# Sliding-window attention with sinks and a SwiGLU block: a range test of the softmax reciprocals and a branch at the end of the program

## The chip, the cores and the metric

The kernel runs on one core of one Trainium2 chip. Times are device microseconds of one launch. A core has five engines with instruction streams of their own: TensorE (PE; its weight loads are listed apart as PEld), VectorE (DVE), ScalarE (ACT), GpSimd (POOL) and SyncE (SP). They wait for each other and for DMA transfers through semaphores. An engine that issues a DMA goes on at once; the transfer raises a semaphore when it has landed.

## What is computed

Attention over 4 batches, 8 heads, 768 positions and heads of 64, in which each query sees the first 4 positions (the sinks) and the last 128 positions up to itself, and then a SwiGLU block on the 3072 resulting rows of 512:

```python
scores = np.where(is_sink | in_window, scale * q @ k.T, -1e9)
a = np.exp(scores - max(scores));  a = a / (sum(a) + 1e-9);  x = a @ v
out = (silu(x @ w_gate) * (x @ w_val)) @ w_out      # 512 -> 1536 -> 512
```

Queries and keys are drawn at a tenth of unit size, so the scores are small. The kernel takes the exponentials without subtracting each row's maximum.

## The kernel before, in words

**Attention** is done in 12 groups of 256 query rows (three per batch). For a group, `step_S` makes the scores, transposed, with their exponentials on ScalarE (L295) and the mask as a product on VectorE (L300); `step_K` makes the sinks' scores (L316). `step_PV` multiplies the exponentials with the values, four heads at a time. The value tiles have a column of ones beside the 64 values of a head, so the sum of the exponentials comes out as the 65th column of the product `po`. `step_PV` then takes the reciprocal of that column (L359: a tile `rcp` of 128x4 from the pool `smallp`, with four buffers) and scales the product by it into `xn` (L365 on VectorE, L362 on ScalarE). `step_X` transposes `xn` into `xT`. There are 48 such reciprocals: 12 groups, two halves of 128 rows, two halves of the heads.

**The SwiGLU block** works on eight row blocks (`SIZES`: 256, 256, 256, 512, 512, 512, 512, 256). `gate` makes one 128x512 piece of the hidden layer: two products on TensorE (L416, tiles `pg` and `pv`), a tanh on ScalarE (L436), two operations on VectorE (L444, L455). `down` makes 128 rows of the output: 12 matmuls (L496, tile `pd`), a copy out of PSUM (L501 on ScalarE; L503 on VectorE for the last 128 columns of the last rows) and a store (L504), which SyncE issues for the later row blocks. PSUM has eight banks, which all tiles of TensorE's results take in turn (`bank`).

**The order** is written out by hand. `weave` goes through a list of `gate` and `down` steps and hands each the attention steps of its slot; `down` spreads what it is handed evenly among its 12 matmuls. Each engine runs its instructions in the order in which this recording makes them. The last list has 24 steps: 12 `gate` steps of row block 6, 6 of row block 7, four `down` of block 6 (steps 18 to 21) and two of block 7. Its attention steps end in slot 9, so steps 10 to 23 are SwiGLU alone.

**The end.** After its last instruction each engine goes to an end block. There SyncE waits, one after the other, for the semaphores of all DMAs and engines; then all engines meet in a barrier, POOL clears the semaphores, and they meet again.

Of the kernel before, what the change touches and what calls it, by code (L numbers as in the profile page):

```python
# [6 lines left out]

FP32 = mybir.dt.float32
BF16 = mybir.dt.bfloat16
AF = mybir.ActivationFunctionType  # L10
ALU = mybir.AluOpType
# [3 lines left out]
def kernel(  # L15
# [12 lines left out]
    nc = tc.nc  # L28
    P = 128
    B, H, S, D = q.shape  # L30
    NS = int(n_sink)
    W = int(window)
    DM = moe_w_gate.shape[0]
# [3 lines left out]
    DMC = DM // P  # L37
    DFC = DF // P
    NP2 = H // 2
    GC = S // 256  # L40
    NG = B * GC
# [6 lines left out]
    FCH = [2] * 6  # L48
    FOF = [(i, f - sum(FCH[:i])) for i in range(len(FCH))
           for f in range(sum(FCH[:i]), sum(FCH[:i + 1]))]  # L50
    scale = 1.0 / float(D) ** 0.5

    def pool(name, bufs, psum=False):
        if psum:
            return ctx.enter_context(
                tc.tile_pool(name=name, bufs=bufs, space=bass.MemoryType.PSUM))
        return ctx.enter_context(tc.tile_pool(name=name, bufs=bufs))

    const = pool("const", 1)
    wpool = pool("wpool", 1)  # L60
    rowp = pool("rowp", 3)
    natp = pool("natp", 1)
    vpool = pool("vpool", 1)
    kqtp = pool("kqtp", 2)
    epool = pool("epool", 2)
    espool = pool("espool", 2)
    xnp = pool("xnp", 4)
    smallp = pool("smallp", 4)
    xtp = pool("xtp", 3)
    tpool = pool("tpool", 3)  # L70
    upool = pool("upool", 3)
    hpool = pool("hpool", 2)
    opool = pool("opool", 4)
# [4 lines left out]
    def bank(shape, dtype, name):  # L78
        return psum.tile(shape, dtype, tag="b", name=name)


    rows, nats, vas = {}, {}, {}
# [43 lines left out]
    wgs, wvs, wos = [], [], []  # L126
# [17 lines left out]
    ident = const.tile([P, P], BF16)  # L144
# [5 lines left out]
    tq = const.tile([P, P], FP32)  # L150
    tk = const.tile([P, 1], FP32)
# [3 lines left out]
    warmed = const.tile([P, 1], FP32)  # L155
    KW = 32
    kss = const.tile([P, B, NP2, KW + 2 * NS], BF16)
    vsbs = []

    nc.vector.memset(zero, 0.0)  # L160
# [45 lines left out]
    def flush():  # L206
        for f in later:
            f()
        later.clear()
# [114 lines left out]
    def step_sinks(g):  # L324

        b, c = divmod(g, GC)
        for j in range(2):
            for hh in range(2):
                r = slice(32 * (2 * j + hh), 32 * (2 * j + hh + 1))
                pos[j, hh] = bank([P, 4, D + 1], FP32, "o")  # L330
                nc.tensor.matmul(pos[j, hh], es_t[g][r], vsbs[b][r], start=True,  # L331
                                 stop=False, skip_group_check=True)

    def step_PV(g, j, hh, norm="v"):
        b, c = divmod(g, GC)
        t = 2 * c + j
        if hh == 0:
            xns[g, j] = xnp.tile([P, DM], BF16, tag="xn", name="xn")
        if c > 0 and j == hh == 0:
            step_sinks(g)  # L340
        po = pos.pop((j, hh)) if c > 0 else bank([P, 4, D + 1], FP32, "o")
        mms = []
        for hq in range(4):
            h = 4 * hh + hq
            if t > 0:
                vp = vas[g][:, 0, h, 0:D + 1] if j else vas[g - 1][:, 1, h, 0:D + 1]
                mms.append((po[:, hq], e_t[g][:, h, 256 * j:256 * j + P], vp))
            mms.append((po[:, hq], e_t[g][:, h, 256 * j + P:256 * (j + 1)],
                        vas[g][:, j, h, 0:D + 1]))
        for i, (o, l, r) in enumerate(mms):  # L350
            nc.tensor.matmul(o, l, r, start=(c == 0 and i == 0),  # L351
                             stop=(i == len(mms) - 1),
                             skip_group_check=True)

        xn = xns[g, j][:, 256 * hh:256 * (hh + 1)].rearrange("p (h d) -> p h d", h=4)

        def dve():
            rcp = smallp.tile([P, 4, 1], FP32, tag="rcp", name="rcp")
            nc.vector.reciprocal(rcp, po[:, :, D:D + 1])  # L359
            if norm == "a":  # L360
                for hq in range(4):
                    nc.scalar.activation(  # L362
                        xn[:, hq], po[:, hq, 0:D], AF.Copy, scale=rcp[:, hq])
            else:
                nc.vector.tensor_tensor(  # L365
                    xn, po[:, :, 0:D], rcp.broadcast_to([P, 4, D]), op=ALU.mult)
        if norm == "a":
            dve()
        else:
            later.append(dve)  # L370
# [135 lines left out]
    def gates(tb):  # L506
        return [(gate, tb, f) for f in range(0, DFC, 512 // SIZES[tb])]
# [4 lines left out]
    def A(fn, *a):  # L512
        return lambda: fn(*a)
# [4 lines left out]
    def Ss(g):  # L518
        return [A(step_S, g, p2) for p2 in range(2)]

    def PVs(g):
        return [A(step_PV, g, j, hh) for hh in range(2) for j in range(2)]

    def Xs(g):
        return [A(step_X, g, j) for j in range(2)]
# [11 lines left out]
    def K(g):  # L537
        return A(step_K, g)

    def weave(us, slots):  # L540
        assert all(i < len(us) for i in slots)
        for i, (fn, tb, x) in enumerate(us):
            fn(tb, x, slots.get(i, []))

    def slots(*pairs):
        sl = {}
        for at, steps in pairs:
            for i, step in zip(at if isinstance(at, tuple) else (at,) * len(steps),
                               steps):
                sl.setdefault(i, []).append(step)  # L550
        return sl
# [106 lines left out]
    later[:0] = masks1  # L658
    flush()

    g0, g1, g2 = gates(0), gates(1), gates(2)
    us = [(gate_held, *g0[0][1:]), (gate_first, *g0[1][1:]), g1[0], g1[1],
          *((gate, "01", f) for f in range(4, DFC)),
# [25 lines left out]
    def pair(ga, gb, sh=0):  # L689
# [15 lines left out]
    us = gates(6) + gates(7) + downs(6) + downs(7)  # L705
    us[-1] = (lambda tb, t, a: down(tb, t, a, True), *us[-1][1:])
    weave(us, slots(
        ((0, 2), Ss(11)), (0, [K(11)]), ((4, 5, 6, 7), PVs(11)), ((8, 9), Xs(11))))


# [33 lines left out]
```

## Time and profile before

| what | value |
|---|---|
| median of 3 runs | 238.3 us (237.76 to 238.68) |
| span of the profiled execution, first to last instruction | 235.8 us (235.84) |
| busy: PE, DVE, ACT, POOL | 229.0, 157.7, 113.6, 74.9 us |
| mean granted TensorE clock | 0.999 |
| L359 reciprocals, 48 | 8.3 us busy, 1.0 us idle before them |
| L496 matmuls | 64.5 us busy |
| instruction packets: q8 / q14 | 15, 0.25 MB / 8, 0.07 MB |

How to read it: the span is one execution seen by the profiler, and the runs are timed without it; no time of the profiled execution is listed other than its span. The page's second part cuts the span into 40 slices with the busy share of each engine in tenths. The chain follows the work that ended last backwards, from each instruction to what released it. A row of the timeline gives the start, the length, the engine, the line, the operation, and how long the engine stood idle before it and for whom. Waits on semaphores, register instructions and branches are not counted as busy; where they are spoken of, the times are those of their records in the same trace, from the span's start.

### The profile page before, as it was taken

How to read it: one execution, taken by the hardware profiler on the slowest of the kernel's cores; microseconds unless marked ns; L12 is line 12 of the kernel's file. 1: busy time of each engine (PE TensorE's matmuls, PEld its weight loads, DVE VectorE, ACT ScalarE, POOL GpSimd, SP SyncE). 2: the span in 40 equal slices, each digit the busy share in tenths (PEclk: the TensorE clock that was granted, in tenths of full speed). 3: DMA queues.
4: the chain of work that ended last, by engine and by line, in shares of the span. 5: the costliest groups of instructions: out<-in, count | busy, mean ns of one | idle time of the engine just before them, and what ended most of it. 6: DMA issues, size and time to landing. Idle time of an engine off the chain costs nothing.

```text
span 235.8 us, 4879 instructions
## 1 busy us (share of the span) xinstructions
PE 229.0 (97%) x1867; PEld 127.7 (54%) x1893; DVE 157.7 (67%) x333; ACT 113.6 (48%) x235; POOL 74.9 (32%) x100
## 2 busy tenths in 40 slices
PE   8999999999999999999999999999999999999994
PEld 5768545795555654444445444445444445488443
DVE  4998888768660988950888970698960598877000
ACT  4884495367453826423836522755522653333221
POOL 8995874724403209105325350080000000000000
PEclk9999999999999999999999999999999999999999
DMA  8999999995995929957989997599414100200132
GB/s 138 165 183 176 182 200 204 159 147 81 166 227 164 148 47 88 156 112 160 137 114 133 137 132 185 126 89 101 81 25 150 50 3 0 45 4 0 48 131 91
DMA packets 108743, 27.62 MB, mean 117 GB/s; under 512 B 95792, under 2 KB 105776, under 8 KB 108720
## 3 DMA queue, kind: packets, MB, share of 16 engines
q0 software_dynamic: 76640, 13.90, 76.4%
q1 hardware_dynamic: 30672, 11.58, 25.4%
q10 hardware_dynamic: 1408, 1.84, 2.5%
q8 instruction: 15, 0.25, 0.5%
q14 instruction: 8, 0.07, 0.1%
HBM read 28.34 MB, written 6.29 MB: 147 GB/s over the span
## 4 chain that ended last, share of the span: by engine, by line
PE 93%; DVE 3%; ACT 1%; issue 1%; DVEq 0%; ACTq 0%
PE pv L416 26%; PE pd L496 26%; PE pg L416 26%; PE o L351 4%; PE s L288 4%; PE w L556 1%; DVE xn L365 1%; PE pt L226 1%; PE o L331 1%; PE pt L572 1%; PE pn L241 1%; PE pk L316 1%; ACT th L436 1%; DVE rcp L359 0%; ACT xn L362 0%
## 5 line engine op out<-in xcount | busy, mean ns | idle before, releaser
L444 DVE SCALAR_TENSOR_TENSOR u<-th,pg 128x512 bf16<-128x512 f32 x72 | 49.2, 683 | 39.2 <-ACT th L436 39.2
L416 PE MATMUL pg<-xT,wg 128*128 128x512 bf16 (+1 forms) x353 | 73.5, 336 | 0.7
L436 ACT ACTIVATE th<-pg 128x512 f32<-128x512 f32 x72 | 43.5, 604 | 63.0 <-PE pg L416 58.2
L416 PE MATMUL pv<-xT,wv 128*128 128x512 bf16 (+1 forms) x349 | 72.9, 336 | 0.6 <-ACT e L295 0.2
L496 PE MATMUL pd<-wo,ht 128*128 128x512 bf16 (+2 forms) x292 | 64.5, 371 | 0.5 <-issue 0.2
L416 PEld LDWEIGHTS <-wg 128*128 128x128 bf16 x360 | 35.0, 98 | 27.9 <-issue 0.4
L455 DVE TENSOR_TENSOR ht<-u,pv 128x512 bf16<-128x512 bf16 x62 | 42.7, 688 | 9.4 <-PE pv L416 2.5
L295 ACT ACTIVATE e<-s 128x512 bf16<-128x512 f32 (+1 forms) x88 | 42.8, 581 | 3.9 <-PE s L288 3.7
L496 PEld LDWEIGHTS <-ht 128*128 128x128 bf16 x300 | 27.9, 98 | 30.3 <-issue 0.3
L416 PEld LDWEIGHTS <-wv 128*128 128x128 bf16 x360 | 32.1, 97 | 20.4 <-issue 1.6
L501 ACT ACTIVATE ot<-pd 128x512 f32<-128x512 f32 (+1 forms) x24 | 14.3, 596 | 46.7 <-PE pd L496 40.7
L111 POOL DMA_DIRECT2D nat<-in_k_dram x20 | 17.7, 890 | 39.7 <-DMA qT<-nat 35.8
L300 DVE TENSOR_TENSOR e<-e,mask 128x1024 bf16<-128x1024 bf16 (+1 forms) x44 | 27.2, 653 | 3.7 <-ACT e L295 3.7
L122 POOL DMA_DIRECT2D va<-in_v_dram x24 | 21.5, 919 | 5.5 <-DMA wo<-in_moe_w_out_dram 2.5
L365 DVE TENSOR_TENSOR xn<-o,rcp 128x256 bf16<-128x256 f32 x44 | 18.7, 424 | 1.5
L351 PEld LDWEIGHTS <-e 128*128 128x128 bf16 x352 | 15.0, 98 | 7.9 <-issue 0.2
L111 POOL DMA_DIRECT2D nat<-in_q_dram x20 | 17.7, 899 | 1.1 <-DMA wg<-in_moe_w_gate_dram 0.5
L351 PE MATMUL o<-va,e 128*128 128x65 bf16 x352 | 17.1, 194 | 0.1
L288 PE MATMUL s<-qT,kT 64*128 64x128 bf16 (+1 forms) x240 | 12.9, 238 | 0.0
L288 PEld LDWEIGHTS <-kT 64*128 64x128 bf16 x240 | 7.7, 94 | 7.3 <-issue 6.4
L503 DVE TENSOR_SCALAR ot<-pd 128x128 f32<-128x128 f32 x1 | 0.3, 292 | 14.3 <-PE pd L496 14.3
L359 DVE RECIPROCAL rcp<-o 128x4 f32<-128x4 f32 x48 | 8.3, 175 | 1.0 <-PE o L351 0.9
(74 smaller groups left out, 93.7 us busy)
## 6 DMA issues: line engine op xcount, KB each, us to landing
out_dram<-ot SPq DMA_DIRECT2D x17, 256.0 KB
va<-in_v_dram POOLq DMA_DIRECT2D x24, 128.0 KB, 6.4
nat<-in_k_dram POOLq DMA_DIRECT2D x20, 128.0 KB, 4.4
nat<-in_q_dram POOLq DMA_DIRECT2D x20, 128.0 KB, 5.9
wg<-in_moe_w_gate_dram POOLq DMA_DIRECT2D x6, 256.0 KB, 7.8
wv<-in_moe_w_val_dram POOLq DMA_DIRECT2D x6, 256.0 KB, 8.4
wo<-in_moe_w_out_dram POOLq DMA_DIRECT2D x4, 384.0 KB, 11.1
out_dram<-ot ACTq DMA_DIRECT2D x6, 256.0 KB
```

Source lines behind the costliest of these rows:

```text
L111: nc.gpsimd.dma_start(x[:, i, j].rearrange("p (h d) -> p h d", d=D), src[b, :, t0:t0 + P].rearrange("h p d -> p h d"))
L122: nc.gpsimd.dma_start(va[:, j, :, 0:D], v[b, :, t0:t0 + P].rearrange("h p d -> p h d"))
L288: nc.tensor.matmul(pss[2 * pp + h][:, col:col + n], kTs[b][r, p, kk:kk + P], qTs[b][r, p, qq:qq + n], start=True, stop=True)
L295: nc.scalar.activation(e_t[g][:, h0 + h, lo:512], pss[2 * pp + h][:, lo:512], AF.Exp, scale=scale)
L300: nc.vector.tensor_tensor(e, e, m[:, :, lo:512].broadcast_to([P, 2, 512 - lo]), op=ALU.mult)
L351: nc.tensor.matmul(o, l, r, start=(c == 0 and i == 0), stop=(i == len(mms) - 1), skip_group_check=True)
L365: nc.vector.tensor_tensor(xn, po[:, :, 0:D], rcp.broadcast_to([P, 4, D]), op=ALU.mult)
L416: nc.tensor.matmul(ps[:, i * n:(i + 1) * n], ws[fi][:, c, fo * P:(fo + 1) * P], xTs[tb][:, c], start=(c == 0), stop=(c == DMC - 1))
L436: nc.scalar.activation(th, pg, AF.Tanh, scale=0.5)
L444: nc.vector.scalar_tensor_tensor(u, th, 1.0, pg, op0=ALU.add, op1=ALU.mult)
L455: nc.vector.tensor_tensor(hts[tb][:, f:f + 512 // SIZES[tb]].rearrange("p a n -> p (a n)"), u, pv, op=ALU.mult)
L496: nc.tensor.matmul(po, hts[tb][:, f, ts * P:(ts + 1) * P], wos[f // n][:, f % n, lo:hi], start=(f == 0), stop=(f == DFC - 1))
```

## The change

The reciprocals go into one table, `rcps`, of 128 x 48 x 4 numbers that lives through the whole program; the pool `smallp` is gone. A new step, `guard`, stands in slot 19 of the last list, which is the second `down` of row block 6, so ahead of its seventh matmul. It clips the 192 reciprocals of each partition to the range from 2^-16 to 2^16, compares with the unclipped, takes the minimum over the row (1 where all are in range), sums over the partitions with a product with a column of ones, and writes 1 into `flag` if the sum is under 127.5. After the last `down`, all engines read `flag` into a register and branch. If it is set, `general` computes the whole output anew in loops over batches and tiles of 128 rows, with each row's maximum taken off the scores; else nothing more is done. In the built program, the loops' instructions stand between the branch's other arm (which holds waits and a jump) and the end block.

```diff
+from concourse.expressions import smax, smin
...
-    smallp = pool("smallp", 4)
...
+    rcps = const.tile([P, 4 * NG, 4, 1], FP32)
+    flag = const.tile([P, 1], mybir.dt.int32)
...
         def dve():
-            rcp = smallp.tile([P, 4, 1], FP32, tag="rcp", name="rcp")
+            rcp = rcps[:, 4 * g + 2 * j + hh]
             nc.vector.reciprocal(rcp, po[:, :, D:D + 1])
...
+    LIM = 2.0 ** 16
+
+    def guard():
+
+        n = 16 * NG
+        x = rcps.rearrange("p g h o -> p (g h o)")
+        c = tpool.tile([P, 512], FP32, tag="th", name="clip")
+        ok = upool.tile([P, 512], BF16, tag="u", name="ok")
+        nc.vector.tensor_scalar(
+            c[:, 0:n], x, 1.0 / LIM, LIM, op0=ALU.max, op1=ALU.min)
+        nc.vector.tensor_tensor(c[:, 0:n], c[:, 0:n], x, op=ALU.is_equal)
+        nc.vector.tensor_reduce(ok[:, 0:1], c[:, 0:n], mybir.AxisListType.X, op=ALU.min)
+        ones = vas[0].rearrange("p j h v -> p (j h) v")[:, :, D]
+        n1 = bank([P, 1], FP32, "n")
+        nc.tensor.matmul(
+            n1[0:2 * H], ones, ok[:, 0:1], start=True, stop=True, skip_group_check=True)
+        nc.vector.tensor_scalar(flag[0:1], n1[0:1], P - 0.5, None, op0=ALU.is_lt)
+
+    def general():
...
+        with tc.For_i(0, B) as b:
+            with tc.For_i(0, S // P) as t:
+                tile_general(b, t, idf, bias)
+
+    def tile_general(b, t, idf, bias):
...
     weave(us, slots(
-        ((0, 2), Ss(11)), (0, [K(11)]), ((4, 5, 6, 7), PVs(11)), ((8, 9), Xs(11))))
+        ((0, 2), Ss(11)), (0, [K(11)]), ((4, 5, 6, 7), PVs(11)), ((8, 9), Xs(11)),
+        (19, [guard])))
+
+    with tc.If(nc.values_load(flag[0:1, 0:1], min_val=0, max_val=1) != 0,
+               preferred_fallthrough_block=False):
+        general()
```

## What the change was expected to do, before it ran

> **What bounds the kernel now.** I read the page's first two parts, then its chain, then the tail of the merged chain in order of time, and last the records of SyncE around the end.
>
> ```profile
> PE 229.0 (97%) x1867; PEld 127.7 (54%) x1893; DVE 157.7 (67%) x333; ACT 113.6 (48%) x235; POOL 74.9 (32%) x100
> ...
> PE   8999999999999999999999999999999999999994
> ...
> PEclk9999999999999999999999999999999999999999
> ...
> q8 instruction: 15, 0.25, 0.5%
> q14 instruction: 8, 0.07, 0.1%
> ...
> PE 93%; DVE 3%; ACT 1%; issue 1%; DVEq 0%; ACTq 0%
> ```
>
> TensorE is busy in every slice and holds 93% of the chain, so whatever adds PE time adds to the span at full price, and whatever sits on another engine costs nothing until the last matmul. The last slice is the exception: PE drops to 4. The end of the program is a stretch of its own, and the change puts its wait there.
>
> The chain in order of time, its last two rows, and VectorE and SyncE in the last 19 us:
>
> ```profile
> 217.57 10.74 PE pd L496 x49
> 228.37 4.52 PE pd L496 x32
> ```
> ```profile
> 217.10 0.69 DVE L444 SCALAR_TENSOR_TENSOR u<-th,pg 128x512 bf16<-128x512 f32 x1 [0.27 <-ACT th L436]
> 217.89 0.69 DVE L455 TENSOR_TENSOR ht<-u,pv 128x512 bf16<-128x512 bf16 x1
> 232.91 0.29 DVE L503 TENSOR_SCALAR ot<-pd 128x128 f32<-128x128 f32 x1 [14.34 <-PE pd L496]
> ```
> ```profile
> 220.56 13.01 SPq L504 DMA_DIRECT2D out_dram<-ot  x7
> ```
>
> From 217.1 on only the six output projections run. VectorE is empty from 218.58 to 232.91. PE ends near 232.9, L503 at 233.2, and SyncE issues the last store (record at 233.23, 0.335 long, so to 233.57). The 2.27 us from there to 235.84 are the end block. Its records on SyncE: six waits on DMA semaphores that pass at once, one per 0.062 us (233.61 to 233.92); a wait that the store before last releases at 234.64; one that the last store releases at 234.87, which is 1.64 us after its issue began; one more wait, two drains (235.00, 235.07). Then the other engines, idle till then, are let through two barriers with a clearing of semaphores (0.139 us) between, to 235.84. So in the tail **SyncE arrives last**, and TensorE, ScalarE and VectorE wait for it for about 2 us.
>
> **The change, part by part.**
>
> 1. *The table* `rcps` in place of the pool `smallp`. The same 48 reciprocals, with the same waits in the order of the instructions; only the address written differs. Cost 0. What could it free? L359 stood idle 1.0 us in all, 0.9 of it for PE, and its share of the chain is 0%; the bound is 0 to 1.0 us and I take 0.
>
> 2. *Guard on VectorE.* Three operations on 128x192 f32 (clip, equality, minimum), queued behind L455, without a wait on PE. Nearest rows: L200 128x128 f32 at 286 ns, L606 a reduction at 205 ns, L444 128x512 at 683 ns. Three times about 0.35 is 1.1 us, so done at about 219.7. The guard stands ahead of the seventh matmul of the second projection: 217.14 + 18 x 0.216 = 221.0 (12 matmuls take 2.59 us). The cover is 1.3 us; if it were gone, PE would wait for the excess. The last comparison, one element from PSUM, fits the empty 14 us ahead of L503. Cost 0.
>
> 3. *Guard on TensorE.* One load of 128x16 weights (tile 128*32) and one matmul of one column, amid loads of 128*128. The trace has such a switch of tile: around L316 (128*32) at 184.6, PE leaves about 0.09 us between the last matmul of the shape before and the first load, and 0.095 us on the way back.
>
> ```profile
> L316 PEld LDWEIGHTS <-kss x64: 92/94/97, 14.5 to 184.6; 128*32 128x32 bf16 x64
> L316 PE MATMUL pk<-qT,kss x64: 218/224/231, 14.5 to 184.7; 128*32 128x128 bf16 x64
> ```
>
> Two switches of 0.1 and one matmul slot of 0.05 (the L351 pairs follow each other at 0.052) make **0.25 us**, all on the path. Lower bound 0.05 (a slot alone), upper 0.45 (switches at the 0.2 us apiece that loads of L316 waited at most). The bank that `n` takes moves the following projections' banks by one; their first matmuls then wait for PE's own earlier work instead of VectorE's, both long past: 0. A switch delays everything behind it by the same 0.25, the last store too.
>
> 4. *The branch.* Every engine gets a register load of `flag` (it waits for the guard's comparison, true since about 221.5), a compare and a branch. On PE, ScalarE, VectorE and POOL, nothing is queued behind but the barrier at which they wait about 2 us today: covered up to that. On SyncE it lies behind the last store and ahead of the end block. Between them stand, by the order of the built program: the load, two register instructions, the compare, then in the untaken arm eight waits (one per hardware DMA semaphore, each raising it), a branch over the general path, and in the end block 12 waits where 9 stood. The ones before were paid for by the store's flight; now **all 12 come after it**. Price of one sequencer step: 0.062 us.
>    The load is not in the trace of before. Lower bound: one step, 0.06. Upper bound: a whole store from issue to release, 1.64. The nearest row is that store less the 0.335 us of writing descriptors, since both are a round trip to memory that no engine work shortens: I take 1.3 us.
>    With 1.3: 233.57 + 1.3 = 234.87; three steps 235.06; eight waits (the store has landed) 235.56; branch 235.62; twelve waits 236.36; two drains, arrival 236.43 instead of 235.07: **+1.36 us**. With 0.06 the load hides behind the flight: released 234.87, then one wait, branch, twelve waits and drains end at 235.87: +0.80. With 1.64: +1.70.
>
>    The Trainium skill (DMA: Bandwidth & Descriptors, Latency and other measured facts) gives a floor of about 0.6 us for a register load. By that figure the sum would be about 1.1 us, an estimate from that page; no row here shows it.
>
> 5. *Clearing* 25 semaphores instead of 20: 0.139 x 25/20, +0.03.
>
> **Sum:** 0.25 + 1.36 + 0.03 = 1.64. The span goes from 235.84 to about 237.5. The page's execution has no other time listed; the median of the runs, 238.3, lies 2.5 above its span, and I keep that difference. **238.3 + 1.6 = 239.9 us, +0.7%.** About 0.5%, 1.2 us, is what a measurement of this kernel can tell from no change.
>
> **Rivals.**
>
> *A: the jump misses its code.* The general path lies between the untaken arm and the end block: some 330 instructions on PE, 175 on VectorE, 115 on SyncE. Instructions arrive in packets: PE's 15 packets for 3760 instructions are 251 each, at 0.94 to 1.38 us; the other engines' are half as large, at 0.31 to 0.64. A target that is not on the chip costs a fetch; the nearest whole price is the store's 1.64 us, for PE about 0.7 more. On SyncE it is wholly exposed: 1.64 + 1.64 = +3.3, 241.6 us. On PE (232.9 + 0.25 + 2.3 = 235.5) or VectorE (233.2 + 0.25 + 1.6 = 235.1) it hides under SyncE's 236.7. For it: PE jumps more than a packet. Against it: packets come ahead of need, PE's last at 228.2, and SyncE jumps fewer instructions than one packet of its own size holds (half of 251). A miss that costs double, 3.3 or more, would show on PE as well, at 236.5 or later.
>
>    The Trainium skill (Runtime: NRT & Kernel Launch, Instruction fetch mechanics) says that a taken branch to outside a window of two pages stalls for a fetch. The packet sizes here agree with paging; by that rule VectorE, whose target is the page after next, would stall, SyncE not, and the sum would stay at 1.6.
>
> *B: the load is cheap.* At 0.7 us or less it lies wholly under the last store's flight; with a guard of 0.05 to 0.25, the time is 0.9 to 1.1 longer: 239.3, within 0.5%. For it: one word. Against it: every access from SyncE to memory in this trace shows more.
>
> *C: faster.* The 48 reciprocals no longer share four buffers. If the idle 1.0 us ahead of L359 were for such a buffer and passed on to PE, it would give up to 1.0 us back, and with end costs at their least (0.80 + 0.05 + 0.03 = 0.88) the time would be 238.2, at best 0.1 lower. It decides only where the end costs less than what is freed. Against it: 0.9 of the 1.0 is put down to PE, and the chain has L359 at 0%.
>
> *D: the branch is taken.* Then 24 tiles run one after the other, each with loads, eight heads in series and a whole projection; one tile cannot be under the 4.4 us in which a `nat` load lands, so over +100 us. Against it: sums of at most 132 exponentials of small scores, so reciprocals between 2^-16 and 2^16.
>
> **How the numbers follow.** Forecast 0.55, A 0.20, B 0.22, C 0.02, D 0.01. The forecast spreads by its bounds from +0.9 (least load, least switch) to +2.2 (1.70 + 0.45 + 0.03); about 0.07 of its 0.55 falls below 1.2 us. Slower by over 0.5%: 0.48 + 0.20 + 0.01 = 0.69. Within: 0.07 + 0.22 = 0.29. Faster: 0.02. The range takes in B's cheap end and most of A: 239.0 to 241.8.
>
> **What would show it.** One matmul of tile `n` near 221.1, every later row of PE about 0.25 later, and the projections otherwise as before: step 3. Three DVE rows between 218.6 and 219.8, and no PE wait for `ok`: step 2. L503 at 233.2 instead of 232.9, and from its end to the span's end 4.0 us instead of 2.6: step 4. If the instruction queues show more packets after 233 than before, and an engine reaches the barrier after SyncE, it is A. If the tail is longer by only 0.8, it is B. The forecast is wrong if the register load on SyncE is well over 1.6 us, or if the register instructions between load and branch cost more than a step each.

## The result, and the profile after

The change makes the kernel slower: 241.12 us (median of 5 runs, 240.95 to 242.07) against 238.04 us for the kernel before (5 runs, 237.76 to 238.68). The ratio is 1.0136, interval 1.0119 to 1.0152, so +3.1 us. Some executions fall in a slower state of the chip; the times given here and below are of executions in the fast state. The profiled execution's span is 239.52 us instead of 235.84, +3.68. The page after, in the rows that answer to those of before:

```profile
PE 229.3 (96%) x1868; PEld 127.9 (53%) x1894; DVE 158.6 (66%) x337; ACT 113.6 (47%) x235; POOL 74.9 (31%) x100
...
PE   8999999999999999999999999999999999999990
...
PEclk9999999999999999999999999999999999999996
...
q8 instruction: 16, 0.26, 0.4%
q14 instruction: 12, 0.10, 0.1%
...
PE 91%; DVE 3%; ACT 1%; issue 1%; DVEq 0%; ACTq 0%
```

TensorE's busy time grew by 0.3 us only, but its digit in the last slice fell from 4 to 0: the whole last slice of 6 us is now tail. One more packet of TensorE's code was fetched (q8) and four more of the other engines' (q14).

The guard first. This is the timeline after, around the guard and the last copy (start, length, engine, line, operation):

```profile
218.75 0.25 DVE L671 TENSOR_SCALAR clip<-rcps 128x192 f32<-128x192 f32 x1
219.04 0.36 DVE L673 TENSOR_TENSOR clip<-clip,rcps 128x192 f32<-128x192 f32 x1
219.43 0.36 DVE L674 TENSOR_REDUCE ok<-clip 128x1 bf16<-128x192 f32 x1
...
221.38 0.19 PE L677 MATMUL n<-ok,va 128*16 128x1 bf16 x1
...
233.40 0.29 DVE L505 TENSOR_SCALAR ot<-pd 128x128 f32<-128x128 f32 x1 [11.64 <-PE pd L498]
```

VectorE is done with the guard at 219.79, and TensorE reaches its matmul without a wait for it. Around that matmul the distance between two matmuls of the projection is 0.432 us (221.068 to 221.500) instead of 0.216, so the guard costs TensorE 0.22 us. The last copy, L505, starts 0.48 later than before. 0.22 of it is the guard; the other quarter of a microsecond is there 10 us into the span already, where no instruction of the guard or the branch has run. I take it for a difference between executions and not for a step of the change: in the profile of the experiment e2 below, which has the table and the whole branch, that copy starts at 232.83, earlier than in before.

The rest, 3.2 us, lies behind the last copy. From its start to the end of the span was 2.93 us (232.91 to 235.84) and is now 6.13 (233.40 to 239.52). I call this stretch the **tail**. Each tail in this document is that of one profiled execution; pairs of kernels in which nothing in the tail differs came out within 0.2 us (2.93 in before and 2.89 in e1; 6.13 in after and 6.30 in e2). The records of the branch's line after (engine's queue, instruction, count, shortest/median/longest in ns, first and last start):

```profile
L844 SPq EVENT_SEMAPHORE  x8: 17/17/17, 235.1 to 237.3; - x8
...
L844 PEldq COMPARE_BRANCH  x2: 90/249/408, 232.2 to 233.6; - x2
...
L844 DVEq COMPARE_BRANCH  x2: 51/53/55, 234.0 to 234.2; - x2
L844 SPq COMPARE_BRANCH  x2: 43/48/53, 235.0 to 237.4; - x2
...
L844 SPq TENSOR_LOAD <-flag x1: 488/488/488, 234.1 to 234.1; - x1
```

and of the end block, after and then before:

```profile
L877 SPq EVENT_SEMAPHORE  x14: 17/28/28, 237.9 to 239.5; - x14
...
L877 SPq DRAIN  x3: 7/7/13, 238.6 to 238.9; - x3
...
L877 PEldq DRAIN  x2: 8/40/72, 234.0 to 239.0; - x2
L877 DVEq DRAIN  x2: 10/26/41, 237.3 to 239.0; - x2
```
```profile
L739 SPq EVENT_SEMAPHORE  x11: 17/28/28, 233.6 to 235.8; - x11
...
L739 SPq DRAIN  x3: 7/7/13, 235.0 to 235.3; - x3
```

Each engine has two branches: the first tests the flag, the second jumps over the general path. A drain is the first thing that every engine but SyncE does in the end block, so the gap from its second branch to its first drain tells whether its code was there. TensorE jumps at 233.55 and drains at 234.02: nothing stands. VectorE's jump ends at 234.28 and it drains only at 237.29: it stands 3.0 us. SyncE's eight waits begin at 235.07, one per 0.07 to 0.08 us, and end at 237.3: the seventh of them, the one for the last store, holds it until 237.215. It then jumps (237.351 to 237.876), goes through twelve waits (to 238.639) and drains; 238.708, its second drain, is its arrival at the barrier, 1.4 us after VectorE. So SyncE is still the last. The tail step by step:

| step | before | after | difference |
|---|---|---|---|
| last copy's start to the store's issue | 0.32 | 0.32 | 0 |
| store's issue to the release of SyncE's wait | 1.64 | 3.50 | +1.86 |
| that release to SyncE's arrival at the barrier | 0.20 | 1.49 | +1.30 |
| barriers and clearing | 0.77 | 0.82 | +0.04 |
| tail | 2.93 | 6.13 | +3.20 |

The third row is a jump of 0.53 and twelve waits at 0.064. The second row is the surprise: the same store of the same 64 KB takes 1.86 us longer. The traffic in that time, by windows of the trace (stretch, length, busy time of the five engines, granted clock, share of the DMA engines' time, GB/s):

```profile
234.05:234.95 0.90, 0.00 (x0) 0.00 (x0) 0.00 (x0) 0.00 (x0) 0.00 (x0) 1.00 0.82 287
234.95:236.15 1.20, 0.00 (x0) 0.00 (x0) 0.00 (x0) 0.00 (x0) 0.00 (x0) 0.80 0.08 21
236.15:236.60 0.45, 0.00 (x0) 0.00 (x0) 0.00 (x0) 0.00 (x0) 0.00 (x0) 0.50 0.07 8
236.60:237.80 1.20, 0.00 (x0) 0.00 (x0) 0.00 (x0) 0.00 (x0) 0.00 (x0) 0.50 0.00 0
```

The store's bulk in before, for comparison, and the time behind it:

```profile
233.50:234.40 0.90, 0.00 (x0) 0.00 (x0) 0.00 (x0) 0.00 (x0) 0.00 (x0) 1.00 0.84 287
234.60:235.70 1.10, 0.00 (x0) 0.00 (x0) 0.00 (x0) 0.00 (x0) 0.00 (x0) 0.81 0.00 0
```

In the first stretch after, the 16 engines carry the store, as in before. Then one engine in the mean is busy (0.08 of 16 is 1.3), for 1.2 us, and then again one, to 236.6. By the packets' own records, the second stretch is mainly one packet of 16 KB of TensorE's code (q8), from 235.07 to 236.12, with one of 8 KB of another engine's code (q14) beside it, from 235.31 to 235.82. The third is nine packets of the last store, eight rows of 512 B and the 4 B that raise its semaphore; all its others had ended by 234.92. The nine start at 236.10, as the 16 KB packet ends. SyncE is released 0.64 us after they end. The records of the store's semaphore say the same: of its 16 increments, 15 are there by 235.28 and the last at 237.20.

### The profile page after: what moved, and what is told of

Its sections match the earlier page's. It is cut to its first block, busy times and chain, and to the rows that moved or that the text cites. A ratio compares the mean times of both kernels' runs of the same rounds, so it can differ in the third digit from the quotient of the medians.

```text
span 239.5 us, 4920 instructions
## 1 busy us (share of the span) xinstructions
PE 229.3 (96%) x1868; PEld 127.9 (53%) x1894; DVE 158.6 (66%) x337; ACT 113.6 (47%) x235; POOL 74.9 (31%) x100
## 4 chain that ended last, share of the span: by engine, by line
PE 91%; DVE 3%; ACT 1%; issue 1%; DVEq 0%; ACTq 0%
PE pd L498 26%; PE pv L418 26%; PE pg L418 25%; PE o L353 4%; PE s L290 4%; PE w L558 1%; DVE xn L367 1%; PE pt L228 1%; PE o L333 1%; PE pt L574 1%; PE pn L243 1%; PE pk L318 1%; ACT th L438 1%; DVE rcps L361 0%; ACT xn L364 0%
## 5 line engine op out<-in xcount | busy, mean ns | idle before, releaser
L367 DVE TENSOR_TENSOR xn<-o,rcps 128x256 bf16<-128x256 f32 x44 | 18.7, 424 | 1.5
L361 DVE RECIPROCAL rcps<-o 128x4 f32<-128x4 f32 x48 | 8.3, 175 | 1.2 <-PE o L353 1.1
```

Of the source, the lines that this page charges most:

```text
L367: nc.vector.tensor_tensor(xn, po[:, :, 0:D], rcp.broadcast_to([P, 4, D]), op=ALU.mult)
```

## Theory and rivals

**Theory.** When an engine jumps into a new packet of its code, it asks, so I suppose, for the packet behind it too. TensorE's jump at 233.55 asks for 16 KB that it does not wait for (it drains at 234.02, before they come); they reach one of the 16 DMA engines ahead of the last store's rows there, and the store lands 1.9 us late. The other half is what stands on SyncE behind that store: jump and twelve waits, 1.3 us. VectorE's stand of 3.0 us is hidden behind both.

**Rival 1, flag late:** the cost is the way of `flag` from PSUM to the registers. **Rival 2, VectorE's stand** holds up the program. **Rival 3, the store is late for itself:** its queue, its bank or its buffers moved, whatever code is fetched.

## The experiments on the change itself

Four kernels shared a chip and the runs of the kernel before, 237.90 us.

**e1: the table and the guard, no branch.**

```diff
-    with tc.If(nc.values_load(flag[0:1, 0:1], min_val=0, max_val=1) != 0,
-               preferred_fallthrough_block=False):
-        general()
```

> Table and guard, without the branch and the general path. Theory (the guard costs one switch of tile on TensorE, 0.22 us, and the rest of the 3.1 us is the tail): 238.0 + 0.2 to 0.5 = 238.2 to 238.5, and from the start of the last VectorE copy to the end of the span 2.9 us as before. Rival (table and guard disturb the attention stages, 0.25 us were already late at 10 us of the span): 238.6 or more, with the delay ahead of the guard.

Measured: 238.04 us, ratio 1.0007 (0.999 to 1.0025); tail 2.89 us, store 1.60 from issue to release. That is 0.14 over the kernel before, under the 0.2 to 0.5 I had expected. Table and guard together can't be told from nothing, and the tail is the one of before.

**e2: the branch alone.** The flag is set to 0 at the start; there is no guard, and the branch and the general path are whole.

```diff
+    nc.vector.memset(flag, 0)
...
-        ((0, 2), Ss(11)), (0, [K(11)]), ((4, 5, 6, 7), PVs(11)), ((8, 9), Xs(11)),
-        (19, [guard])))
+        ((0, 2), Ss(11)), (0, [K(11)]), ((4, 5, 6, 7), PVs(11)), ((8, 9), Xs(11))))
```

> Branch and general path as in the change; no guard, the flag is set to 0 at the start of the program, so the branch is never taken and nothing is tested. Theory (the tail carries the cost): 238.0 + 2.7 to 3.0 = 240.7 to 241.0, the last store released about 3.5 us after its issue. Rival (the wait for a flag written late costs): 239.5 or less, because the flag is there from the start.

Measured: 240.89 us, ratio 1.0132 (1.0116 to 1.0149); tail 6.30, store 3.66:

```profile
L844 SPq EVENT_SEMAPHORE  x8: 17/17/17, 234.5 to 236.9; - x8
```

The flag is known 230 us before SyncE reads it, and the cost is all there: rival 1 is out. 0.14 (e1) and 2.99 (e2) make 3.13, and the whole change measured 3.08.

**e3 and e4: a near and a far jump of TensorE.** The general path is replaced by dummy matmuls, 20 or 140, so that no other engine has anything to jump over; the recomputation is left out.

```diff
-        general()
+        fill(20, bank([P, 512], FP32, "w"))
```

and with `fill(140, ...)`.

> The change, with the general path replaced by 40 instructions on TensorE alone (20 weight loads and matmuls of zeros), so that every engine's jump lands near; the output is no longer made anew where the test fails. Theory (TensorE's code packet, fetched when its jump enters another page, occupies a DMA engine on which rows of the last store wait): no packet on TensorE's instruction queue after the last projection, the last store released 1.6 to 1.8 us after its issue, and 238.0 + 0.2 (guard) + 1.0 (register load, waits in a row after it) = 239.2 to 239.5. Rival (the register loads and branches themselves are the cost): 240.5 or more, the release still 3.5 us after the issue.

> As the run with 40 instructions, but with 280 on TensorE (140 weight loads and matmuls of zeros), the other engines' jumps still near; the output is no longer made anew where the test fails. Theory: a packet of 16 KB on TensorE's instruction queue about 1.5 us after its branch, the last store released about 3.5 us after its issue, and 240.2 to 240.6, about 1 us above the run with 40. Rival (cost of the register loads and branches, or of the other engines' code): the same time as the run with 40, within 0.2 us.

Measured: e3 238.81 us, ratio 1.0045 (1.0028 to 1.0061), tail 3.51. That is lower than the 239.2 to 239.5 I had expected. What it has over before is SyncE's way through load, registers and compare: it begins the twelve waits at 235.2, when most of the store's flight is over, and ends them at 236.0. e4 239.74 us (three runs, 239.69 to 240.35), ratio 1.0078 (1.0058 to 1.0099), tail 4.88. That is under the expected 240.2 to 240.6 too. Between them stand 0.93 us of median and 1.37 us of tail, for the length of TensorE's jump alone. The instruction queues, e3 and then e4:

```profile
q8 instruction: 15, 0.25, 0.4%
```
```profile
q8 instruction: 16, 0.26, 0.4%
```

And the DMA windows after the last store's bulk, again e3 and then e4:

```profile
234.00:234.90 0.90, 0.00 (x0) 0.00 (x0) 0.00 (x0) 0.00 (x0) 0.00 (x0) 1.00 0.83 291
234.90:236.10 1.20, 0.00 (x0) 0.00 (x0) 0.00 (x0) 0.00 (x0) 0.00 (x0) 1.00 0.00 0
```
```profile
236.40:236.95 0.55, 0.00 (x0) 0.00 (x0) 0.00 (x0) 0.00 (x0) 0.00 (x0) 0.50 0.07 7
```

With the near jump the sixteenth packet is never asked for, nothing moves after 234.90, and the store's packets are done 1.52 us after the copy's start. With the far jump the packet is there (from 234.97, 1.48 us long), the last nine packets of the store come behind it, in the window shown, and the store takes 3.55 us. Of the 16 increments of its semaphore 15 are there by 235.57 and the last at 237.53; with the near jump all 16 are there by 235.27. No engine stands in e4: VectorE has almost nothing to jump. No 8 KB packet is fetched in e4's tail either, so the one in after is not needed for the delay. So rivals 2 and 3 don't make this part.

e4 also separates the theory's second half. SyncE has no waits to do in e4's untaken arm, since the dummy path holds no DMA, and is through its other waits before the store lands. Its tail is 0.32 + 3.55 + 0.20 + 0.81 = 4.88, where the 0.20 from release to arrival is as in before. The whole change's tail is 1.25 longer than that: the 1.30 of the third row of the table, less the 0.05 by which its store is earlier.

## The experiments on the engines' parts

The next seven kernels stand on a ground of their own: all transposes are made by TensorE (in before and after, most are made by DMA transfers), and dummy matmuls and memsets near the start place TensorE's and VectorE's last instructions within their packets as they are in after. The ground takes some 280 us, at a mean granted clock of 0.96, and its runs scatter by 3.7 us. So the tails are compared, not the medians. f1 to f4 ran on one chip, g1 to g3 on another.

**f1 and f2: the ground without and with the change.**

```diff
+    junk = const.tile([P, 1], FP32)
...
-                t0 = c * 256 + j * P
-                nc.sync.dma_start_transpose(
-                    (kTs, qTs)[i][b][:, :, t0:t0 + P], nats[g][:, i, j])
+                step_TN(g, i, j)
...
-        if g not in PEX:
-            def sp():
-                nc.sync.dma_start_transpose(xTs[tb][:, :, off:off + P], xns[g, j])
-            later.append(sp)
-            return
...
-    fill(14, bank([P, 512], FP32, "w"))
+    fill(74, bank([P, 512], FP32, "w"))
+    for _ in range(108):
+        nc.vector.memset(junk, 0.0)
```

> The kernel before, with all transposes on TensorE instead of by DMA (SyncE issues none), and with 60 matmuls and 108 one-column memsets more at the start, so that TensorE's and VectorE's code stands at the same place in its packets at the branch as in the change. A ground for the next runs: the stages ahead of the tail are longer, the tail is the same. Expected by all theories: 8 to 30 us above the kernel before, and from the start of the last VectorE copy to the end of the span 2.9 us, the last store released 1.64 us after its issue.

> The change on that ground. Theory (the tail carries the cost, whatever the stages ahead of it do): 2.7 to 3.3 us above the ground, the last store released 3.3 to 3.7 us after its issue, VectorE 3.0 us behind its jump. Rival (the cost hangs on the DMA transposes or on SyncE's longer queue): under 2.3 us above the ground.

Measured: f1 281.25 us (277.85 to 281.6), tail 3.05, store 1.65. It lies 43 us above the kernel before, not 8 to 30; why was not followed up. f2 285.02 us (283.84 to 286.68), tail 8.95, store 3.64. The late store is there again; the tail misses the 6 us I expected, and the medians lie 3.8 apart, not 2.7 to 3.3. SyncE's drains in f1:

```profile
L735 SPq DRAIN  x3: 7/7/7, 278.2 to 278.5; - x3
```

SyncE's records in f2:

```profile
L840 SPq COMPARE_BRANCH  x2: 38/44/49, 275.0 to 277.6; - x2
```
```profile
L873 SPq EVENT_SEMAPHORE  x14: 17/28/28, 278.1 to 282.3; - x14
...
L873 SPq DRAIN  x3: 7/7/7, 281.1 to 281.7; - x3
...
L873 DVEq DRAIN  x2: 10/34/58, 277.1 to 281.7; - x2
```

SyncE jumps at 277.63, makes the end block's first two waits at 278.12 and 278.21, and the third only at 280.44. It stands 2.2 us where nothing is to be waited for. A reading that fits: the jump lands two instructions ahead of the end of a packet, and the packet behind is asked for only on entry. An 8 KB packet starts 1.05 us after the jump (278.67 to 279.20), and SyncE goes on 1.2 us after its end, 2.8 us after the jump. Neither the theory nor a rival had this. By this reading it depends on where the end block's instructions fall in the packets, and in after, where SyncE doesn't stand, they fall well. No run moved SyncE's instructions alone to test it.

**f3: only VectorE has something to jump over.** The general path is 170 memsets; the recomputation is left out.

```diff
-        general()
+        for _ in range(170):
+            nc.vector.memset(one, 1.0)
```

> On that ground, the change with the general path replaced by 170 memsets on VectorE and nothing else; the output is no longer made anew where the test fails. VectorE's jump lands as far as in the change, the other engines' near. Theory (VectorE's target is beyond the packet fetched ahead, so it stands for a whole fetch, with no packet of TensorE's in the way): VectorE goes on about 3.0 us after its jump and reaches the barrier after SyncE, so it ends the program: 1.7 to 2.1 us above the ground, the last store released after 1.6 to 1.8 us. Rival (VectorE's stand in the change was due to TensorE's packet or to the late store): 0.8 to 1.1 us above the ground, as with TensorE near, VectorE at the barrier before SyncE.

Measured: 278.10 and 280.38 us (two runs), which the scatter doesn't set apart from the ground; tail 4.86, 1.81 over the ground's, in the expected 1.7 to 2.1.

```profile
L840 DVEq COMPARE_BRANCH  x2: 51/53/55, 274.4 to 274.6; - x2
...
L840 SPq COMPARE_BRANCH  x2: 38/44/49, 275.3 to 275.4; - x2
```
```profile
L874 SPq DRAIN  x3: 7/7/120, 276.4 to 278.3; - x3
L874 DVEq DRAIN  x2: 10/34/57, 277.6 to 277.9; - x2
```

VectorE's jump ends at 274.62 and it drains at 277.58, after 2.97 us, while SyncE is through at 276.4 and waits for it. No packet of TensorE's code is fetched in this tail, so the stand is VectorE's own. By the packets' records an 8 KB packet starts 1.19 us after the start of the jump and takes 0.36, and VectorE goes on 1.46 after its end. With everything else short the stand ends the program (0.2 of the 1.81 us lies in longer barriers behind it): rival 2 has a real cost, and in after it is only hidden.

**f4: TensorE's place in its packet.** Twelve dummy matmuls ahead of the branch move TensorE's jump, and nothing else.

```diff
+    fill(12, bank([P, 512], FP32, "w"))
     with tc.If(nc.values_load(flag[0:1, 0:1], min_val=0, max_val=1) != 0,
```

> On that ground, the change with 12 matmuls of zeros (256 columns, 1.3 us in all) on TensorE between its last projection and its branch. Theory (TensorE's packet meets the last store): the packet starts about 1.3 us later, after the store's rows are written, so the store is released 1.6 to 1.8 us after its issue though TensorE has more to do; VectorE, 3.0 us behind its jump, reaches the barrier last: 1.5 to 2.0 us above the ground, 1.0 to 1.6 below the change there. Rival (the store is late for another reason, or the packet delays it wherever it falls): at the change's time or above.

Measured: 285.13 us, tail 6.88. TensorE's code packet starts 2.54 us after the copy instead of 1.44, the store's packets are all done by 1.58, and the store is released 1.70 us after its issue, near the ground's 1.65. The DMA windows behind the store's bulk; the code packet falls in the second:

```profile
276.85:277.70 0.85, 0.00 (x0) 0.00 (x0) 0.00 (x0) 0.00 (x0) 0.00 (x0) 1.00 0.04 10
277.70:279.10 1.40, 0.00 (x0) 0.00 (x0) 0.00 (x0) 0.00 (x0) 0.00 (x0) 0.97 0.07 18
```

The meeting is gone, though the packet is still fetched. The total misses all the same: the tail is 3.83 over the ground, not 1.5 to 2.0, and the median is f2's within 0.2 us. SyncE's waits in the untaken arm end early, but the end block has f2's stand again (278.12 to 280.22):

```profile
L841 SPq EVENT_SEMAPHORE  x8: 17/17/17, 276.9 to 277.4; - x8
```
```profile
L874 SPq EVENT_SEMAPHORE  x14: 17/28/28, 278.0 to 282.0; - x14
L874 SPq DRAIN  x3: 7/7/7, 280.9 to 281.5; - x3
```

**g1: nothing for SyncE to jump over.** The general path's loads and stores are issued by GpSimd.

```diff
-            nc.sync.dma_start(
+            nc.gpsimd.dma_start(
...
-        nc.sync.dma_start(out[bass.ds(b * S + t0, P)], ot)
+        nc.gpsimd.dma_start(out[bass.ds(b * S + t0, P)], ot)
```

> On the ground with all transposes on TensorE, the change with one edit: the general path's loads and stores are issued by GpSimd instead of SyncE. SyncE then has one branch in place of eight waits in the untaken arm, no address registers, and a jump over 62 instructions instead of 123; GpSimd's longer path runs while it is idle. Theory (SyncE's own instructions after the store's release and its far jump are their share of the tail): from the start of the last VectorE copy to the end 4.7 to 5.0 us, against 8.95 for the change on this ground, in which SyncE stood 2.6 us at its jump; the store is still released 3.5 us after its issue, by TensorE's packet. Rival (the waits and registers are paid for anyway by the late store): 6.9 or more.

Measured: 283.0 us (2 runs), tail 5.09, just over the expected 4.7 to 5.0; store still 3.65.

```profile
L873 SPq EVENT_SEMAPHORE  x14: 17/28/28, 277.5 to 280.4; - x14
...
L873 SPq DRAIN  x3: 7/7/7, 279.6 to 279.9; - x3
```

The eight waits of the untaken arm are gone, SyncE is in the end block at 277.5 and stands nowhere but at the store. The tail is 0.32 + 3.65 + 0.31 + 0.82. Of f2's 8.95 us 3.86 are gone: 3.5 between the store's release and SyncE's arrival at the barrier, the rest in the barriers, which took 1.18 in f2. The late store stays, as the theory says, because TensorE's jump is as it was.

**g2: three remedies together.** g1's edit, f4's twelve matmuls, and 43 of the general path's instructions moved from VectorE to ScalarE and GpSimd, so that VectorE jumps over 129 instructions instead of 169.

```diff
-            nc.vector.tensor_copy(out=dst, in_=pt[:, :, 0:n])
+            nc.scalar.copy(out=dst, in_=pt[:, :, 0:n])
...
-        nc.vector.memset(vt[:, :, :, D:D + 1], 1.0)
+        nc.gpsimd.memset(vt[:, :, :, D:D + 1], 1.0)
...
+    fill(12, bank([P, 512], FP32, "w"))
```

> On that ground, three edits together, with the change's function: the general path's DMAs on GpSimd, 12 matmuls of zeros ahead of TensorE's branch, and 43 of the general path's instructions moved from VectorE to ScalarE and GpSimd, so that VectorE skips 129 and not 169. Theory (each stand has its own cause: packet on the store's DMA engine, target beyond the next packet, waits after the release): tail 3.4 to 3.8 us against 3.05 of the ground, the store released after 1.6 to 1.8 us of its issue or found landed, no engine standing at its jump. Rival for VectorE (any jump past a packet stands): tail 4.9, as with 170 memsets.

Measured: 281.49 us (278.61 to 281.89), tail 3.83, at the upper edge of the expected 3.4 to 3.8.

```profile
L841 DVEq COMPARE_BRANCH  x2: 51/53/55, 276.5 to 276.7; - x2
```
```profile
L874 DVEq DRAIN  x2: 10/24/38, 277.3 to 279.1; - x2
...
L874 SPq EVENT_SEMAPHORE  x14: 17/28/28, 278.0 to 279.6; - x14
L874 SPq DRAIN  x3: 7/7/7, 278.8 to 279.1; - x3
```

VectorE's 3 us are gone (jump at 276.7, drain at 277.3), the store's last packets are done 2.00 us after the copy's start, before SyncE asks for them, and SyncE goes from 278.0 to 278.8 through its waits without a stand. The branch costs 0.78 us of tail here instead of 5.90. It is the least that was reached with the whole general path kept. It stays above the kernel without a branch, and on this ground 0.78 us can't be told from the scatter of the runs, so no median is claimed for it. The store isn't quite free of code here either: its last nine packets start at 277.65, just as an 8 KB packet ends, 0.23 us after its others. So an engine other than TensorE may do the same on a smaller scale; that is read from the times and not tested.

**g3: the path taken.** g2 with the flag's test turned round, so that the general path is executed.

```diff
-        nc.vector.tensor_scalar(flag[0:1], n1[0:1], P - 0.5, None, op0=ALU.is_lt)
+        nc.vector.tensor_scalar(flag[0:1], n1[0:1], P - 0.5, None, op0=ALU.is_gt)
```

> The run with three edits, its comparison turned round, so that the test fails on these inputs and the general path is taken; it computes the whole output a second time. Both theories: the fourth rival's price, over 100 us above the ground; with 24 tiles one after the other of some 280 instructions on TensorE, each head waiting for VectorE and ScalarE in turn, an estimate of 20 to 40 us a tile, 500 to 1000 us in all.

Measured: 1812.1 us (2 runs); the mean granted clock was 0.641. That is about 1530 us for 24 tiles, 64 us a tile, well above the 20 to 40 I had expected. The code behind the branch is slow when it is wanted, too. TensorE's longest waits in it, 348 us in all, are for ScalarE's exponentials; the rest of the 64 us a tile was not followed up.

## Why the prediction was right or wrong

**The direction and the place were right.** The cost sits behind the last copy, SyncE carries it, and the time lies in the range. The size was not: +3.1 us where the forecast had +1.6. That 241.12 still lies in the range is luck: the forecast's own bounds end at +2.2, and the range goes up to 241.8 only because it takes in most of rival A, whose mechanism, SyncE standing for a fetch, did not happen.

**Step 1, the table:** 0, and e1 shows no difference.

**Steps 2 and 3, the guard:** right. VectorE's three operations took 1.04 us (218.75 to 219.79) where 1.1 was predicted, and TensorE lost 0.22 where I took 0.25. The trace has the guard's matmul as a tile of 128*16, not 128*32.

**Step 4, the branch, is the step that failed**, in the sentence that let the last store land 1.64 us after its issue as before. It took 3.50, +1.86. I had laid the register load's length beside the store's flight as if the two were independent of all else that the branch starts, and had put the branches of the idle engines at nothing, as covered by the barrier. But the branch also starts TensorE's fetch, and e3, e4 and f4 show the fetch in the store's way: no packet, no delay; a packet, a delay; a packet 1.1 us later, no delay.

The terms within step 4 were mis-sized too, partly against each other:

- The register load took 0.49 us on SyncE (0.47 to 0.54 on the five engines), not 1.3, so it lay wholly under the flight. Rival B was right about that, not about the time. The Trainium skill (DMA: Bandwidth & Descriptors, Latency and other measured facts) gives a floor of about 0.6 us; the five loads here are all under it.
- Register instructions, assertion and compare took about 0.42 us, from the load's end near 234.59 to 235.01, not 0.19. Hidden as well.
- The jump took 0.53 us on SyncE, not 0.06. This one lies behind the store and is paid in full.
- Twelve waits behind the store: 0.763 us, or 0.064 apiece, against the 0.74 predicted. Right. The eight waits, predicted behind the load, came before the landing but for two.

With the 1.64 us flight, the store would have released SyncE at about 235.35 in after, before SyncE comes to that wait by its own step (235.51); jump, waits and barriers as measured then give a tail of about 4.4 us, +1.5. So the wrong load and the wrong jump nearly made each other good, and without the late store the forecast of +1.36 for the tail would nearly have stood, by luck. This is worked out from the rows, not run.

**Step 5, the clearing:** 0.139 to 0.177 us, +0.04 against +0.03. Right.

**Rival A** had the right subject, code that isn't there, and the wrong place. It looked for an engine that stands at its jump; SyncE did not stand in after. VectorE did, 3.0 us and not the estimated 1.64, hidden as the rival said it would be. The cost came as traffic instead, from TensorE, whose own jump went well. That its price, +3.3, is close to the measured +3.1 is luck too. The rival's own mark, more packets after 233, was in the page (16 and 12 instead of 15 and 8), but its other mark, an engine later than SyncE at the barrier, was not.

The rule of the Trainium skill (Runtime: NRT & Kernel Launch, Instruction fetch mechanics), that a taken branch out of a window of two pages stalls for a fetch, named the right engine: in after VectorE stood, 3.0 us, and SyncE did not. What it says of a stall doesn't reach the cost found here, which falls on another engine's store.

**Rivals C and D:** nothing was freed (e1: ratio 1.0007), and the path isn't taken; it would have cost some 1530 us.

**What stays open.** The records used don't number the DMA engines. That the code packet and the store's last rows share one is inferred, from close evidence: one increment of 16 is late, the rows join the packet's end to 0.02 us in after, e2, e4, f2 and g1, and they part when the packet is moved or taken away. What that engine did between the end of the store's other rows and the start of the packet's record (0.15 us in after, 0.38 in g1) the records don't show; nor whether the packet is the one of the jump's target or the one behind it, only that TensorE did not wait for it. Why a jump to code that is there costs SyncE half a microsecond (0.53 in after and 0.48 in g1, against 0.19 in e3, from the second branch to the first wait) was not tried.

## What to carry to other kernels

At a program's end, follow the jump of every engine, the idle ones too: ask which packet of code it will fetch, and which transfer that packet meets. Keep out of the stream of the engine that awaits the last store whatever would come after its landing, waits and jumps alike. Code that is rarely run was cheap to skip here where it was short on each engine (TensorE fetched no packet over 40 instructions and one over 280; VectorE did not stand over 129 and did over 170), and where its DMAs were issued by an engine that had nothing to do at the end.

## What the runs showed of the chip that was not expected

- The record of a 16 KB packet of TensorE's code in the tail is 0.95 (g1) to 1.57 us (e2) long, 1.05 in after. A store whose last rows come behind it is released 3.5 to 3.7 us after its issue (after, e2, e4, f2, g1) instead of 1.6 to 1.7 (before, e1, f1, f4).
- Where VectorE jumps over some 170 instructions it stands 2.9 to 3.0 us (after, e2, f2, f3, f4, g1). SyncE stands 2.1 to 2.2 us two waits behind its jump in f2 and f4; that it landed just ahead of a packet's end is inferred.
- Reading one word into a register takes 0.47 to 0.59 us over all engines and runs (0.49 on SyncE in after), about a third of the last store's flight in before.
